# A conformer block on one core: gated unit and conv in 128 + 16 channels, paired scores, and a reordered start

## Chip, cores and metric

One NeuronCore of a Trainium2 chip. The metric is the device time of one execution in microseconds (us), lower is better. "Granted clock" is the share of full speed that TensorE got. The engines are PE (TensorE, matmuls), PEld (its weight loads), ACT (ScalarE), DVE (VectorE), POOL (GpSimd) and SP (SyncE, which issues DMAs here).

## The reference, cut to what matters

```python
B, T, D, K, H = 2, 4000, 144, 5, 4          # bf16 throughout
x = x + 0.5 * silu(ln(x) @ w_ff1a) @ w_ff1b # FF, 576 wide
q, k, v = split(ln(x) @ w_qkv)              # 4 heads of 36
x = x + softmax(q k^T * scale) v @ w_o      # full attention over 4000 tokens
a, b = split(ln(x) @ w_pw1)                 # the gated unit: two halves of 144 channels
h = a * sigmoid(b)
c = sum_i shift(h, i) * dw[i]               # conv over 5 tokens, per channel
x = x + silu(c) @ w_pw2
x = x + 0.5 * silu(ln(x) @ w_ff2a) @ w_ff2b
return ln(x)
```

## The kernel before

Tokens are worked on in 16 chunks of 512 (two of them 416), four blocks of 128 per chunk. The program is written by a small list scheduler in Python: every operation is recorded with an estimated cost, threads of "side work" (FF, projections, gated unit, conv) compete, and the order per engine that comes out is fixed when the kernel is built.

Attention runs as 992 tiles of 128 keys x 512 queries x 2 heads. Most exponentials are on ScalarE; some are computed on VectorE with shifts and a polynomial:

```python
def dve_exp():                              # a VectorE tile
    ...
    for hh in range(2):
        if hh:
            bk = yield need("pe", banks, dur=-0.24)
        s_mm(gi, kt, hh, PSV[:, bk, 0:m], [("ps", bk)], 0.107)   # two 64x64 matmuls of 512 columns
        op("dve", "tensor_scalar", DN[...], PSV[:, bk, 0:m], ...)
        op("dve", "scalar_tensor_tensor", DF[...], ...)
        banks.give(bk)
```

The 144 channels of the gated unit and the conv are worked on as two halves of 72, one channel per row (partition):

```python
def glu(c, s, hf):                          # hf = 0, 1
    ...
    mm2(c, WP1, s, D + hf * HD, D + (hf + 1) * HD, bk, HD, ["WP1"])
    t = yield from tanh(n, bk, HD)          # 72 x 512 on ScalarE
    ...
    mm2(c, WP1, s, hf * HD, (hf + 1) * HD, bk, HD, ["WP1"])
    ...
    op("dve", "scalar_tensor_tensor", out=U[0:HD, c % NU, hf, :, 1:1 + nt], ...)
def conv(c, z, hf, silu):                   # nine matmuls per half, weights are diagonal
    ...
```

The softmax here doesn't subtract the row's maximum and nothing guards it: scores larger than these inputs give would overflow.

Of the kernel before, what the change touches and what calls it, by code (L numbers as in the profile page):

```python
# [6 lines left out]
ALU = mybir.AluOpType  # L7
# [32 lines left out]
class Rec:  # L40
# [7 lines left out]
    def __init__(self, nc):  # L48
        self.nc = nc
        self.ops = []  # L50
        self.n = {}
        self.hist = {}
        self.free = {e: 1.0 for e in self.ENGS}
        self.kind = None
        self.last = 0.0
        self.filler = None

    def op(self, eng, name, *a, r=(), w=(), q=None, cost=0.1, kind=None, **k):
        o = Op()
        o.eng, o.name, o.a, o.k, o.q = eng, name, a, k, q  # L60
        o.deps, o.inc, o.cnt = [], False, 0
        lane = eng if q is None else "q:" + q
        o.idx = self.n.get(lane, 0)
        self.n[lane] = o.idx + 1
        for key in r:
            h = self.hist.setdefault(key, ([], []))
            o.deps += [(d, True) for d in h[0]]
            h[1].append(o)
        for key in w:
            h = self.hist.setdefault(key, ([], []))  # L70
            o.deps += [(d, key[0] in ("DN", "DF", "PD")) for d in h[0] + h[1] if d is not o]
            if h[1] and not (len(h[1]) == 1 and h[1][0] is o):
                self.hist[key] = ([o], [])
            else:
                h[0].append(o)
        start = self.free[eng]
        for d, raw in o.deps:
            if d.eng != eng or d.q is not None or (raw and eng != "pe"):
                start = max(start, d.done)
        if eng == "pe" and kind == "idle":  # L80
            start = self.free["pe"]
        elif eng == "pe":
            gap = start - self.free["pe"]
            if self.filler is not None and gap > 0.3:
                self.fill(int((gap - 0.15) / 0.11), o, lane)
            if kind != self.kind:
                start += 0.13
            self.kind = kind
        self.free[eng] = start + cost
        o.done = start + cost + self.LAT[eng]  # L90
        self.last = o.done
        self.ops.append(o)
        return o
# [186 lines left out]
def bass_standalone__conformer_family_zipformer__speech_kernel(  # L280
# [43 lines left out]
    LEAD = 20  # L324
    NSER = 3
    LATE = 0.8
# [4 lines left out]
    SLACK, MORE, LAG = 0.7, 0.4, 3  # L331
# [24 lines left out]
    U = sb("U", [NU, 2, NB, KTL + 4])  # L356
    SW = sb("SW", [NSW, 2, CH])
# [11 lines left out]
    WP1 = sb("WP1", [2, 2 * D])  # L369
    WP2 = sb("WP2", [2, D])  # L370
    DWR = sb("DWR", [D])
    DWT = sb("DWT", [2, 8], F32)
    DG = sb("DG", [2, KCONV, HD])
# [12 lines left out]
    def load(eng, q, dst, src, w):  # L386
        op(eng, "dma_start", dst, src, q=q, w=w, cost=0.7)
# [19 lines left out]

    load_x("sp", 0)
# [4 lines left out]
    load("sp", "w2", WO[0:HD, :, :], kh(w_o), ["WO"])  # L413
    load("sp", "w2", WP1[0:HD, :, :], kh(w_pw1), ["WP1"])
    load("sp", "w2", WP2[0:HD, :, :], kh(w_pw2), ["WP2"])
    load("sp", "w2", DWR[0:KCONV, :], dw, ["DWR"])
    load_ff("sp", "w2", WA2, WB2, w_ff2a, w_ff2b, "W2")
    for c in range(CPB, NCH):
        load_x("sp", c)

    op("dve", "memset", DUM[:, :], 0.0, w=["DUM"])
    op("pool", "memset", IDENT[:, :], 0.0, w=["ID0"])
# [3 lines left out]
    op("pool", "memset", XN[:, :, :, :, :], 0.0, w=["XN0"], cost=2.0)  # L426
    op("pool", "memset", AN[:, :, :, :, :], 0.0, w=["AN0"], cost=1.0)
    op("dve", "memset", WQ[:, :, :, :], 0.0, w=["WQ0"])
    op("dve", "memset", WK[:, :, :, :], 0.0, w=["WK0"])
    zero_ff(WA1, WB1, "W1")  # L430
    zero_ff(WA2, WB2, "W2")
    op("dve", "tensor_copy", IDF[:, :], IDENT[:, :], r=["ID"], w=["IDF"], cost=0.2)

# [10 lines left out]
    def setup_qk():  # L444
        for Wt, nm, o0 in ((WQ, "WQ", 0), (WK, "WK", D)):
            for k in range(2):
                op("dve", "tensor_copy", Wt[0:HD, k, :, 0:DH],
                   WQKV[0:HD, k, o0:o0 + D].rearrange("p (h d) -> p h d", h=H), r=["WQKV", nm + "0"], w=[nm],
                   cost=0.15)
# [36 lines left out]
    def setup_dw():  # L486
        bk = yield need("pe", banks, dur=0.1)
        for k in range(2):
            op("pe", "transpose", PSH[0:HD, bk, k * 8:k * 8 + KCONV], DWR[0:KCONV, k * HD:(k + 1) * HD],
               IDENT[0:KCONV, 0:KCONV], r=["DWR", "ID"], w=[("ps", bk)], kind="s")  # L490
        yield need("dve")
        op("dve", "tensor_scalar", DWT[0:HD, :, 0:KCONV],
           PSH[0:HD, bk, 0:16].rearrange("p (k n) -> p k n", k=2)[:, :, 0:KCONV], 0.5, None, op0=ALU.mult,
           r=[("ps", bk)], w=["DWT"])
        banks.give(bk)
        for k in range(2):
            yield need("dve")
            for i in range(KCONV):
                op("dve", "tensor_scalar", DG[0:HD, k, i, :], IDENT[0:HD, 0:HD], DWT[0:HD, k, i:i + 1], None,
                   op0=ALU.mult, r=["DWT", "ID"], w=["DG"], cost=0.2)  # L500

# [20 lines left out]
    def transp(c, src, rk, s, g, flat=False):  # L522
# [3 lines left out]
        if not (mode["front"] or mode["tail"] or flat):  # L526
# [3 lines left out]
               src(rows).rearrange("p i k f -> p (i k f)"), q=f"t{s}_{g}", r=rk, w=[("XT", s, g)], cost=0.1)  # L530
# [221 lines left out]
    def glu(c, s, hf):  # L752
        cc = c % CPB
        bk = yield need("pe", banks, dur=0.43)
        n, nt = nc_(c), tb(c)
        mm2(c, WP1, s, D + hf * HD, D + (hf + 1) * HD, bk, HD, ["WP1"])
        t = yield from tanh(n, bk, HD)
        banks.give(bk)
        bk = yield need("pe", banks, dur=0.43)
        mm2(c, WP1, s, hf * HD, (hf + 1) * HD, bk, HD, ["WP1"])  # L760
        yield need("dve")
        op("dve", "scalar_tensor_tensor", out=U[0:HD, c % NU, hf, :, 1:1 + nt],
           in0=TH[0:HD, t, 0:n].rearrange("p (i n) -> p i n", i=NB), scalar=1.0,
           in1=PSV[0:HD, bk, 0:n].rearrange("p (i n) -> p i n", i=NB), op0=ALU.add, op1=ALU.mult,
           r=[("TH", t), ("ps", bk)], w=[("U", c % NU)], cost=0.63)
        banks.give(bk)
        thp.give(t)

    def post1(c, a):
# [20 lines left out]
        if cc == 0:  # L790
            op("pool", "memset", U[0:HD, v, :, 2:4, 0:1], 0.0, w=[("UL", v)], cost=0.1)
        else:
            op("pool", "tensor_copy", U[0:HD, v, :, 2:4, 0:1], U[0:HD, w, :, 2:4, KTL:KTL + 1],
               r=[("U", w)], w=[("UL", v)], cost=0.25)
            op("pool", "tensor_copy", U[0:HD, w, :, 0:2, KTL + 1:KTL + 2], U[0:HD, v, :, 0:2, 1:2],
               r=[("U", v)], w=[("UR", w)], cost=0.25)
        if cc == CPB - 1:
            op("pool", "memset", U[0:HD, v, :, 0:2, n + 1:n + 2], 0.0, w=[("UR", v)], cost=0.1)
        glu_done.add(c)

    def conv(c, z, hf, silu):
        v, n, nt = c % NU, nc_(c), tb(c)
        bk = yield need("pe", banks, dur=1.07)
        o = PSV[0:HD, bk, 0:n].rearrange("p (i n) -> p i n", i=NB)
        u = U[0:HD, c % NU, hf, :, :]
        parts = [(2, 0, 4, 0, 1), (1, 1, 4, 0, 1), (1, 0, 1, 3, 0), (0, 2, 4, 0, 1), (0, 0, 2, 2, 0),
                 (3, 0, 3, 1, 1), (3, 3, 4, 0, 2), (4, 0, 2, 2, 1), (4, 2, 4, 0, 2)]
        for j, (tap, i0, i1, s0, off) in enumerate(parts):
            op("pe", "matmul", o[:, i0:i1, :], lhsT=DG[0:HD, hf, tap, :], rhs=u[:, s0:s0 + i1 - i0, off:off + nt],
               start=j == 0, stop=j == len(parts) - 1, r=[("U", v), ("UL", v), ("UR", v), "DG"], w=[("ps", bk)],  # L810
               cost=0.0525 * (i1 - i0), kind="f", skip_group_check=True)
        if silu:
            yield need("act")
            op("act", "activation", SW[0:HD, z, hf, 0:n], PSV[0:HD, bk, 0:n], ACT.Silu, bias=0.0, scale=1.0,
               r=[("ps", bk)], w=[("SW", z)], cost=0.48)
            banks.give(bk)
            return
        t = yield from tanh(n, bk, HD)
        yield need("dve")
        gate(SW[0:HD, z, hf, 0:n], n, bk, HD, t, [("SW", z)])  # L820
# [3 lines left out]
    def post2(c):  # L824
# [9 lines left out]
        def half(g):  # L834
            yield from residual(
                c, g, lambda i: [(SW[0:HD, z, k, i * n:(i + 1) * n], WP2[0:HD, k, :]) for k in range(2)],
                1.0 if silu else 0.5, [("SW", z), "WP2"])
# [114 lines left out]
    def dve_exp():  # L952
# [4 lines left out]
        while True:  # L957
# [3 lines left out]
            bk = yield need("pe", banks, cond=lambda: stolen() is not None, dur=-0.24)  # L961
# [6 lines left out]
            for hh in range(2):  # L968
                if hh:
                    bk = yield need("pe", banks, dur=-0.24)  # L970
                s_mm(gi, kt, hh, PSV[:, bk, 0:m], [("ps", bk)], 0.107)
# [6 lines left out]
                   cost=0.64)  # L978
# [63 lines left out]
    setup_qk()  # L1042
    for c in range(CPB):
        S.add(ff1(c, True))
# [52 lines left out]
    while n_e < n_s or group() is not None:  # L1097
# [9 lines left out]
        lag = len(att_done) - len(fin)  # L1107
# [4 lines left out]
        if th is not None and (stuck or a is None or t < a or (th.req[0] == "act" and t < a + 0.05)):  # L1112
# [3 lines left out]
            if mode["front"] and len(kv_done) == CPB:  # L1116
                mode["front"] = False
                S.add(setup_dw())
                S.add(series(g for c in range(CPB, NCH) for g in (ff1(c, False), pre2(c))))
# [60 lines left out]
```

## Time and profile before

| what | before |
|---|---|
| runs when first timed | 1069.4, 1081.8, 1082.3 us; profiled run 1072.8 |
| span of the profiled run | 1071.0 us, mean granted clock 0.979 |
| start to first exponential | 55.3 us |
| first to last exponential | 966.4 us |
| last exponential to the end | 49.3 us |

"Middle" below is the second of these stretches, "end" the third; both count from the starts of those exponentials. The view of busy time by stretch gives, for any stretch, its length and each engine's busy us with the instruction count in brackets, in the order PE, PEld, DVE, ACT, POOL, then granted clock, DMA share and GB/s. For the middle of before:

```profile
55.30:1021.70 966.40, 833.11 (x9724) 288.72 (x9724) 674.09 (x1582) 935.08 (x1128) 325.16 (x505) 0.99 0.10 19
```

Subtracting ScalarE's busy time from the length leaves 31.3 us idle: middle = ScalarE's busy time + its idle time.

### The profile page before, as it was taken

The numbers are of one execution on the slowest core, as the hardware profiler recorded it, in microseconds if no ns is written. First come the engines' busy times: TensorE is split into PE (matmuls) and PEld (weight loads), VectorE is DVE, ScalarE is ACT, GpSimd is POOL, SyncE is SP. The second block draws the span as 40 slices with busy tenths as digits, with TensorE's granted clock in tenths as the row PEclk, the third lists the DMA queues.
The fourth block names the chain that finished last, engine by engine and source line by source line (L and its number), as shares of the span: only waits on it lengthen the run. The fifth ranks groups of instructions, "written<-read, shape, count | busy, mean of one in ns | idle before, by whom it ended". The sixth has DMA issues, their size and how long they took to land.

```text
span 1071.0 us, 25080 instructions
## 1 busy us (share of the span) xinstructions
PE 920.2 (86%) x10499; PEld 348.2 (33%) x10499; DVE 745.0 (70%) x1883; ACT 983.2 (92%) x1219; POOL 364.7 (34%) x589
## 2 busy tenths in 40 slices
PE   8998888887989989898888889888888888888886
PEld 4632222222233323233332233322232232333254
DVE  7885378767655675757678886588748877765654
ACT  3698999998999999999999999999999999999952
POOL 5431141404237452653622043520443040515213
PEclk8999999999999999899999999999999999999997
DMA  4000010101012010110100011100101010102000
GB/s 124 2 2 9 13 31 11 26 6 26 16 26 41 19 39 11 26 34 13 31 7 19 1 26 21 27 14 7 25 17 27 1 31 1 27 11 32 12 2 16
DMA packets 76089, 22.29 MB, mean 21 GB/s; under 512 B 73400, under 2 KB 75976, under 8 KB 75976
## 3 DMA queue, kind: packets, MB, share of 16 engines
q1 hardware_dynamic: 74820, 20.22, 9.4%
q8 instruction: 82, 1.34, 0.5%
q10 hardware_dynamic: 1156, 0.47, 0.2%
q14 instruction: 31, 0.25, 0.1%
HBM read 3.30 MB, written 2.30 MB: 5 GB/s over the span
## 4 chain that ended last, share of the span: by engine, by line
ACT 62%; PE 24%; DVE 5%; DMA 3%; POOL 2%; issue 2%; SPq 1%; ACTq 0%; POOLq 0%; DVEq 0%
ACT PT L161 55%; PE PS L161 24%; ACT TH L161 5%; DMA XT<-AN 2%; POOL RS L161 1%; DVE PD L161 1%; ACT HT L161 1%; POOL XN L161 1%; DMA XT<-XN 1%; DVE XN L161 1%; SPq L161 1%; DVE ST L161 1%; DMA WQKV<-in_w_qkv_dram 0%; ACT PR L161 0%; DVE DF L161 0%
## 5 line engine op out<-in xcount | busy, mean ns | idle before, releaser
L161 ACT ACTIVATE PT<-PS 128x1024 bf16<-128x1024 f32 (+1 forms) x932 | 870.0, 1050 | 18.5 <-PE PS L161 16.2
L161 PE MATMUL PS<-QT,KT 64*64 64x512 bf16 (+1 forms) x3968 | 416.7, 396 | 100.7 <-ACT PT L161 90.5
L161 PE MATMUL PS<-PT,VA 64*64 64x512 bf16 (+1 forms) x3728 | 362.3, 377 | 0.6 <-ACT PT L161 0.6
L161 PEld LDWEIGHTS PS<-QT,KT 64*64 64x64 bf16 x3968 | 118.7, 104 | 430.4 <-ACT PT L161 358.9
L161 POOL TENSOR_SCALAR RS<-MV 128x2 f32<-128x2 f32 (+1 forms) x160 | 37.2, 232 | 622.4 <-DVE MV L161 622.3
L161 POOL TENSOR_SCALAR XN<-X,MV,RS 128x144 bf16<-128x144 bf16 (+1 forms) x228 | 203.2, 904 | 5.7
L161 POOL TENSOR_TENSOR RS<-RS,NHALF 128x2 f32<-128x2 f32 (+1 forms) x160 | 115.3, 721 | 13.3
L161 PEld LDWEIGHTS PS<-PT,VA 64*64 64x64 bf16 x3728 | 111.1, 107 | 21.2 <-issue 11.2
L161 DVE SCALAR_TENSOR_TENSOR HT<-TH,PS 128x512 bf16<-128x512 bf16 (+2 forms) x105 | 64.5, 622 | 66.6 <-ACT TH L161 66.4
L161 ACT ACTIVATE TH<-PS 128x512 bf16<-128x512 f32 (+4 forms) x165 | 99.6, 604 | 10.1 <-PE PS L161 9.3
L161 PE MATMUL PS<-XT,WA 72*128 72x512 bf16 (+3 forms) x384 | 91.5, 356 | 13.5 <-issue 6.2
L161 DVE TENSOR_SCALAR DN<-PS 128x512 bf16<-128x512 f32 (+1 forms) x120 | 80.7, 679 | 29.0 <-PE PS L161 27.4
L161 DVE SCALAR_TENSOR_TENSOR X<-PS,X 128x288 bf16<-128x288 f32 (+1 forms) x128 | 57.1, 447 | 41.2 <-PE PS L161 40.8
L161 DVE TENSOR_TENSOR PD<-PD,DF 128x1024 f16<-128x1024 f16 (+1 forms) x120 | 83.2, 694 | 3.6
L161 DVE SCALAR_TENSOR_TENSOR DF<-PS,DN 128x512 f16<-128x512 f32 (+1 forms) x120 | 81.6, 683 | 3.6
L161 DVE BATCH_NORM_STATS2 ST<-X 128x6 f32<-128x144 bf16 (+1 forms) x320 | 81.3, 296 | 3.0
L161 PE MATMUL PS<-WB,HT 128*128 128x144 bf16 (+1 forms) x640 | 51.3, 233 | 2.1 <-ACT HT L161 1.2
L161 PEld LDWEIGHTS PS<-XT,WA 72*128 72x128 bf16 x384 | 29.9, 100 | 70.9 <-issue 33.9
L161 DVE COPY OTA<-PS 128x512 f32<-128x512 f32 (+1 forms) x32 | 21.7, 679 | 40.4 <-PE PS L161 40.4
L161 PEld LDWEIGHTS PS<-WB,HT 128*128 128x128 bf16 (+1 forms) x640 | 42.5, 105 | 19.5 <-issue 5.7
L161 DVE BATCH_NORM_AGGREGATE MV<-ST 128x2 f32<-128x6 f32 (+1 forms) x320 | 44.5, 169 | 0.0
L161 DVE TENSOR_TENSOR PD<-PD,DN 128x1024 uint16<-128x1024 f16 (+1 forms) x60 | 42.8, 719 | 1.7
(76 smaller groups left out, 685.9 us busy)
## 6 DMA issues: line engine op xcount, KB each, us to landing
X<-in_x_dram SPq DMA_DIRECT2D x14, 144.0 KB, 3.3
out_dram<-XN SPq DMA_DIRECT2D x28, 72.0 KB, 1.7
XT<-XN SPq DMA_TRANSPOSE x86, 2.4
XT<-AN SPq DMA_TRANSPOSE x30, 2.5
X<-in_x_dram SPq DMA_DIRECT2D x2, 117.0 KB
out_dram<-XN SPq DMA_DIRECT2D x4, 58.5 KB
WA<-in_w_ff1a_dram ACTq DMA_DIRECT2D x1, 144.0 KB
WB<-in_w_ff1b_dram ACTq DMA_DIRECT2D x1, 144.0 KB
```

The lines of the kernel that those rows point to most:

```text
L161: ins = getattr(eng, o.name)(*o.a, **o.k)
```

## The change

Its intent: columns are what costs and rows next to nothing, so 144 channels go as one pass of 128 rows and one pass in which the last 16 channels of four token blocks are stacked at rows 0, 32, 64 and 96, 128 columns long. The scores of a VectorE tile are issued together, so that all four 64x64 tiles of the array work at once. The first norms no longer stand behind the copies of the QKV weights. With them came new scheduler constants: LEAD (the fewest tiles left in a group that VectorE may take one from), LATE (the lateness that this needs), MORE (slack per lag), NPRE (series in which the second batch is prepared) and AHEAD (how far that runs ahead). The core of the diff:

```diff
-    def glu(c, s, hf):
+    def glu(c, s, rem):
+        if rem:                                   # 16 channels x 4 blocks
+            for k in range(2):
+                for j, w0 in enumerate((2 * D - 16, 128)):
+                    for i in range(NB):
+                        op("pe", "matmul", PSV[32 * i:32 * i + 32, bk, 256 * j:256 * j + nt], ...)
+        else:
+            mm2(c, WP1, s, D, D + 128, bk, 128, ["WP1"])
...
+        if rem:                                   # the conv of the stacked 16 channels
+            n = nt
+            for sh in range(3):
+                op("pe", "matmul", PSV[:, bk, 0:n], lhsT=DR[:, sh, :], rhs=U[:, v, NB, sh:sh + nt], ...)
+        else:                                     # nine matmuls with diagonals of 128 x 128
...
-            bk = yield need("pe", banks, cond=lambda: stolen() is not None, dur=-0.24)
+            bk = yield need("pe", banks, cond=lambda: len(banks.free) > 1 and stolen() is not None, dur=-0.24)
+            bks = (bk, banks.take())
...
-        if not (mode["front"] or mode["tail"] or flat):
+        dma = not (mode["front"] or mode["tail"] or flat)
+        if mode["front"] and not flat and c:
+            yield need("sp")
+            dma = R.free["sp"] < max(R.ready(k) for k in rk) + 0.3
...
-               src(rows)..., q=f"t{s}_{g}", r=rk, w=[("XT", s, g)], cost=0.1)
+               src(rows)..., q=f"t{s}_{g}", r=rk, w=[("XT", s, g)], cost=1.2)
...
-    LEAD = 20                  LATE = 0.8              MORE = 0.4
+    LEAD = 18    NPRE = 2      LATE = 0.2  AHEAD = 0.6 MORE = 0.2
...
-    setup_qk()
     for c in range(CPB):
-        S.add(ff1(c, True))
+        S.add(ff1(c, True), ready=R.ready(("X", c, 0)))
+    S.add(setup_qk(), ready=R.ready("WQKV"))
```

Cut: the buffers, the padded weights, smaller fills, the silu table loaded early, the float32 identity copied later, the weights and second half of x loaded after the start.

## The prediction

> **What bounds the kernel now.** I first read the page's busy shares, then cut the span into three stages with the view of busy time by stretch. The columns there are stretch, length, then busy us and (count) of each engine, the granted clock, the DMA share and GB/s.
>
> ```profile
> PE 920.2 (86%) x10499; PEld 348.2 (33%) x10499; DVE 745.0 (70%) x1883; ACT 983.2 (92%) x1219; POOL 364.7 (34%) x589
> ...
> 0.00:100.00 100.00, 90.69 (x824) 46.97 (x824) 76.12 (x321) 69.02 (x110) 35.64 (x74) 0.97 0.13 34
> 100.00:1010.00 910.00, 784.42 (x9188) 271.88 (x9188) 640.46 (x1453) 884.23 (x1061) 315.69 (x484) 0.99 0.10 20
> 1010.00:1071.00 61.00, 45.05 (x495) 29.37 (x494) 28.37 (x110) 29.99 (x50) 13.37 (x31) 0.88 0.03 8
> ```
>
> The overall 92% of ScalarE hides three regimes. From 100 to 1010 us ScalarE is busy 884.2 of 910 us, 97.2%: it is the bound, and only 25.8 us of idle time are left there. In the first 100 us it is busy 69.0 us, and at the end about half. The waits of ScalarE inside the middle stage (us in total, times, longest) say who is to blame for the rest:
>
> ```profile
> ACT PT L161 <- PE PS L161: 16.2, 32, 2.4
> ACT TH L161 <- PE PS L161: 6.5, 15, 0.8
> ```
>
> 22.7 of the 25.8 us are waits for TensorE. The groups by form say what ScalarE does, and what VectorE pays for the gates:
>
> ```profile
> L161 ACT ACTIVATE PT<-PS 128x1024 bf16<-128x1024 f32 x812 | 776.4, 1070 | 17.2 <-PE PS L161 15.5
> L161 ACT ACTIVATE PT<-PS 128x832 bf16<-128x832 f32 x120 | 94.0, 919 | 1.3 <-PE PS L161 0.8
> L161 ACT ACTIVATE TH<-PS 72x512 bf16<-72x512 f32 x54 | 33.4, 618 | 4.8 <-PE PS L161 4.1
> L161 DVE SCALAR_TENSOR_TENSOR U<-TH,PS 72x512 bf16<-72x512 bf16 x28 | 19.1, 684 | 28.5 <-PE PS L161 25.3 <-ACT PT L161 3.1
> L161 DVE TENSOR_SCALAR PD<-DF 128x1024 f16<-128x1024 f16 x56 | 24.5, 440 | 1.6
> ```
>
> There are 992 exponential tiles (32 groups of 31); ScalarE does 812 + 120 = 932, VectorE the other 60. A full ScalarE tile occupies 776.4/812 = 0.96 us of its time, 0.92 in an unbroken run. So three things shorten the middle: less other ScalarE work, more tiles on VectorE, fewer waits for TensorE. VectorE is idle there for 910 - 640 = 270 us, so it is not the bound.
>
> The start is bound otherwise. From the timeline of the first 15 us (start, duration, engine, instruction, what ended the idle time before it):
>
> ```profile
> 1.44 3.51 POOL L161 MEMSET XN<- 128x4096 bf16 x1
> 2.56 4.21 DVE L161 CAST IDF<-IDENT 128x128 f32<-128x128 bf16 x1
> 4.89 1.81 POOL L161 MEMSET AN<- 128x2048 bf16 x1
> 8.73 0.30 DVE L161 COPY WQ<-WQKV 72x144 bf16<-72x144 bf16 x2 [1.29 <-DMA WQKV<-in_w_qkv_dram]
> 9.17 0.51 DVE L161 BATCH_NORM_STATS2 ST<-X 128x6 f32<-128x144 bf16 x2
> 11.64 0.41 PE L161 MATMUL PS<-IDENT,XN 128*72 128x128 bf16 x4 [0.68 <-DVE XN L161]
> 14.54 3.83 PE L161 MATMUL PS<-XT,WA 72*128 72x512 bf16 x12 [0.29 <-issue]
> ```
>
> The first norm (9.17) stands in VectorE's program behind a cast that takes 4.21 us and a copy that waits for the QKV weights. The data were there before: loads of x take 3.3 us in the median and the first is issued at 0.72, so it landed near 4. After that the first blocks repeat every 4.29 us (first silu of a block at 22.40, 26.69, 30.98, 35.27), and between 20 and 40 us TensorE is busy 19.4 of 20 us: there it is the bound.
>
> **What the Trainium skill says.** "ScalarE: Activation LUTs", section What ACT_TABLE_LOAD costs, gives 186 ns + 0.833 ns per column for an ACTIVATE with immediates, 93 ns of which overlap back to back: 0.95 us for 1024 columns and 0.52 for 512. The chain shows 0.92 and 0.49, so I take its slope with the trace's slots. "SBUF — State Buffer", section Who interferes with whom: the port pair that VectorE's 2-port copies and GpSimd share is an exclusive lock, and the loser waits. The trace fits: the cast of 128 columns ends at 6.77, GpSimd's second fill at 6.70. "TensorE: Matmul & The Clock Gate", section Wait — 56ns, not 53.3ns?: start to start is columns/2.4 GHz + 2.5 ns, 0.216 us for 512 columns, 0.056 for 128. A conv half (9 matmuls, 2560 columns, so 1.09 us) shows 1.06 us of weight loads in the last stage. "TensorEngine Tiling (Array Packing)", section Key Properties: tiles of one array run in parallel, a change of tiling drains. The trace shows four 64x64 score matmuls of 512 columns in 0.41 us from first start to last end, so they do overlap.
>
> **The change part by part.**
>
> *Channels 128 + 16 on ScalarE.* Each of 16 chunks has a gated unit and a conv, each with two activations of 72 rows x 512 columns. They become one of 128 x 512 and one of 128 x 128. Rows are free, columns cost: a slot of 0.49 us for 512 columns shrinks to 0.49 - 384 x 0.000833 = 0.17. A pair goes from 0.98 to 0.66, 0.32 saved, x32 pairs = 10 us, some 28 pairs (9 us) in the middle stage, where ScalarE is the bound and all of it counts.
>
> *The same on VectorE.* A gate of 512 columns is 0.684 us. The rows of HT give 0.683 for 512 and 0.420 for 256, so about 0.29 for 128; a pair saves 0.395, x about 30 = 12 us. VectorE isn't the bound, so this only buys tiles: a tile costs VectorE 2 x 0.686 + 2 x 0.689 + 0.440 + 0.446 + 2 x 0.702 + 0.723 = 5.8 us, so two tiles.
>
> *The same on TensorE.* Conv: 18 matmuls (2.13 us of weight loads in the trace) become 9 and 3 of 128 columns: 1.06 + 0.17, saving 0.9 us x 16 = 14 us. Gated unit: 8 x 0.216 become 4 x 0.216 and 16 narrow ones of 128 columns, 0.22 us if four run side by side, 0.9 if none do: between 0 and 0.65 us x 16, say 5 us. The output product keeps its two terms.
>
> *Paired scores.* A VectorE tile's scores were two pairs of matmuls at different times, two tiles of the array idle each time; now all four go together, 0.43 to 0.22 us, x60 = 13 us of TensorE, and one change of tiling less. The price is that both banks left for side work must be free at once, and the second is held while VectorE works on the first (1.4 us more).
>
> TensorE thus loses some 32 us. None is on ScalarE's clock directly; it reaches the end through the 22.7 us of waits and by letting side work and VectorE tiles in earlier. I take 6 us of the waits.
>
> *More VectorE tiles.* The bar for starting one falls (lateness 0.8 to 0.2, least remaining 20 to 18), TensorE has room, VectorE has 270 idle us. The pairing speaks against it. I choose 60 to about 68: 8 x 0.93 = 7 us, from VectorE's share of the middle rising from 70% to about 74%.
>
> *The start.* The norm goes from 9.17 to about 4.5: fills of 1.65 and 0.9 us of VectorE remain before it and x lands near 4. TensorE can't use all of it: its 36 warm-up matmuls run to 10.96. Transposes go from 11.64 to about 10.9, but then all are ready instead of arriving over 2 us, so the first FF matmul goes from 14.54 to about 12: 2.5 us. The silu table (1.28 us at 14.68) is loaded earlier, perhaps 0.5 us more. Some transposes of later blocks go to DMA: eight on TensorE cost 0.61 us per block in the trace, 14 such sets in the front; if half move, 4 us where TensorE is the bound. The start is worth 7 us.
>
> *The end.* From the last exponential at 1022.8 to 1071 is a chain of single blocks. It holds 2.1 us of conv matmuls in front of the last transposes and two more conv pairs: 3 us.
>
> *Moved loads and two series.* Late weights and the second half of x are issued after the front instead of at 5 to 13 us. They fill the SP queue by some 25 issues x 0.43 us, 10 us around 90 us, when the first transposes of the next stage want it. I charge 1 us.
>
> Sum: 9 + 6 + 7 + 7 + 3 - 1 = 31 us off the profiled span of 1071, so 1040. The runs of before, 1069.4 to 1082.3 with 1072.8 for the profiled one, lie some 6 us over the span on average; 1046 it is, 3% under their mean of 1076.7.
>
> **Rivals.** *The pairing starves side work.* Only two banks serve side work, and a paired tile holds both for its first 1.5 us. Then the tile count stays at 60 or falls, and TensorE's gain becomes waits for banks. For it: those waits already exist (27 us of VectorE waiting before DN). Against: the scheduler asks for both banks free before it starts. Outcome: 1058 to 1064. *TensorE's gain goes straight to the end.* The chain that ended last is PE for 24%, so one might take 24% of 1071 as TensorE-bound and expect 50 us. Against: the same stretches have ScalarE at 96 to 98% busy, so the chain there merely passes through TensorE. Outcome if true: 1025. *VectorE takes many tiles.* At 80% busy, 18 more: 10 us better, 1036. *The start is hidden by the warm-up and weights.* Then its gain is 1 or 2 us: 1051.
>
> **Range and chances.** The firm parts are 9 us of activations, about 3 of the start and 3 of the end: 15 us, 1.4%. Passing 2% (1055) needs some 7 more from tiles, waits and transposes, which I put at 16. I give that 0.74, 0.25 to within 2%, 0.01 to slower. The range is 1028 to 1064.
>
> **What would show it.** In the profile after: 128x128 activations and gates in place of the 72-row ones, ScalarE's time for TH down by some 9 us; PT count down from 932 to about 924; first norm near 4.5 and first FF matmul near 12 us; block period in the front under 4.29 us; conv matmuls 12 per chunk; ScalarE still at 97% or more in the middle. I am wrong if PT goes up, if ScalarE's waits for TensorE grow over 25 us, or if the first exponential comes no earlier than 55.3 us.

## More of the kernel before

Normed blocks are transposed by a DMA issued from SP; the scheduler's estimate of its queue time stands at the end of the line:

```python
op("sp", "dma_start_transpose", XT[:, s, ...], src(rows)..., q=f"t{s}_{g}", r=rk, w=[("XT", s, g)], cost=0.1)
```

## The result, and the profile after

The changed kernel ran at 1030.8, 1034.2 and 1037.1 us in its fast runs (1054.6 in one slow run, at granted clock 0.959, left out); before had a median of 1082.0 over four runs. The ratio is 0.9594 (95% interval 0.948 to 0.971). Every ratio here is the mean of one kernel's fast runs over the mean of before's fast runs of the same rounds, so it is not quite the ratio of quoted medians. The result is correct. The forecast was 1046 us with a range of 1028 to 1064.

The profiled span fell from 1071.0 to 1029.0 us, by 42 us against 31 forecast. The middle of the changed kernel, busy time by stretch as above:

```profile
48.10:988.50 940.40, 797.90 (x9807) 272.30 (x9807) 686.22 (x1645) 922.52 (x1122) 333.17 (x510) 0.99 0.11 23
```

ScalarE is busy 922.5 us (12.6 less than before) and idle 17.9 (13.4 less). The waits of ScalarE for TensorE in this stretch, to be set against the 16.2 and 6.5 us of before (the same in before's whole middle as in the prediction's window):

```profile
ACT PT L165 <- PE PS L165: 8.4, 25, 1.4
ACT TH L165 <- PE PS L165: 3.0, 10, 0.7
```

The account by stretch of the profiled runs:

| stretch | before | after | difference | forecast |
|---|---|---|---|---|
| start to first exponential | 55.3 | 48.1 | -7.2 | -7 |
| middle, ScalarE busy | 935.1 | 922.5 | -12.6 | -16 |
| middle, ScalarE idle | 31.3 | 17.9 | -13.4 | -6 |
| end | 49.3 | 40.5 | -8.8 | -3 |
| moved loads | | in the rows above | | +1 |

The start, from the timeline of the changed kernel (start, duration, engine, instruction, idle time before it and what ended it):

```profile
1.17 9.67 PE L165 MATMUL PS<-DUM 128*128 128x512 bf16 x36 [1.17 <-DVE DUM L165]
...
3.97 0.52 DVE L165 BATCH_NORM_STATS2 ST<-X 128x6 f32<-128x144 bf16 x2
...
10.68 0.61 PE L165 MATMUL PS<-IDENT,XN 128*72 128x128 bf16 x8
...
12.24 2.34 PE L165 MATMUL PS<-XT,WA 72*128 72x512 bf16 x12 [0.50 <-ACT XT L165]
```

The first norm stands at 3.97 us instead of 9.17, the first FF product at 12.24 instead of 14.54. As foreseen, it is the 36 warm-up matmuls that hold it there.

What the split into 128 + 16 channels saves can be read without any contention in the gated unit of the very last chunk (416 tokens). The timeline of before:

```profile
1035.29 0.92 ACT L161 ACTIVATE TH<-PS 72x416 bf16<-72x416 f32 x2 [0.63 <-PE PS L161]
...
1036.45 1.08 DVE L161 SCALAR_TENSOR_TENSOR U<-TH,PS 72x416 bf16<-72x416 bf16 x2
...
1037.88 2.01 PE L161 MATMUL PS<-U,DG 72*72 72x416 bf16 x18
```

and of the changed kernel:

```profile
1001.13 0.67 ACT L165 ACTIVATE TH<-PS 128x416 bf16<-128x416 f32 x2 [0.62 <-PE PS L165]
...
1002.31 0.76 DVE L165 SCALAR_TENSOR_TENSOR U<-TH,PS 128x416 bf16<-128x416 bf16 x2
...
1003.43 1.08 PE L165 MATMUL PS<-U,DG 128*128 128x416 bf16 x9 [0.91 <-POOL U L165]
...
1004.35 0.30 PE L165 MATMUL PS<-U,DR 128*128 128x104 bf16 x3
```

Two activations of 416 columns became one of 416 and one of 104 (the line names only the first shape): 0.92 to 0.67 us, and by the slope of the prediction 312 columns x 0.000833 = 0.26 was due. The gate fell by 0.32 us, the conv matmuls from 2.01 to 1.22 us (first start to last end).

VectorE tiles went from 60 to 65 (exponentials on ScalarE from 932 to 927), where 68 were expected.

The same can be read for the whole middle, by the groups of ScalarE's activations by form, before and then after:

```profile
L161 ACT ACTIVATE TH<-PS 128x512 bf16<-128x512 f32 x76 | 49.1, 646 | 4.0 <-PE PS L161 3.9
L161 ACT ACTIVATE TH<-PS 72x512 bf16<-72x512 f32 x52 | 32.2, 619 | 2.6 <-PE PS L161 1.9
...
L165 ACT ACTIVATE TH<-PS 128x512 bf16<-128x512 f32 x105 | 68.9, 656 | 3.2 <-PE PS L165 2.7
L165 ACT ACTIVATE TH<-PS 128x128 bf16<-128x128 f32 x27 | 9.5, 350 | 0.0
```

Neighbours overlap, so I counted each activation in the traces from the end of the one before it. The gated unit and the conv then cost 27.4 us for 28 pairs before and some 19.5 for 29 pairs after: 0.98 and 0.67 us a pair, where the prediction has 0.98 and 0.66. The exponentials fell from 842.5 to 839.4 us, ScalarE's copies (QT, KT, VA, XT) from 9.8 to 6.9, and the FF's tanh, two more of them, rose by 1.4. These four, -7.9, -3.1, -2.9 and +1.4, make up the 12.6 us to 0.1.

### The profile page after: what moved, and what is told of

It reads as the page before. It is cut to its first block, busy times and chain, and to the rows that moved or that the text cites. A ratio compares the mean times of both kernels' runs of the same rounds, so it can differ in the third digit from the quotient of the medians.

```text
span 1029.0 us, 25199 instructions
## 1 busy us (share of the span) xinstructions
PE 871.0 (85%) x10488; PEld 321.4 (31%) x10488; DVE 749.9 (73%) x1938; ACT 963.6 (94%) x1202; POOL 369.7 (36%) x594
## 4 chain that ended last, share of the span: by engine, by line
ACT 67%; PE 25%; DVE 5%; issue 1%; POOL 1%; DMA 1%; POOLq 0%; DVEq 0%; ACTq 0%; SPq 0%
ACT PT L165 60%; PE PS L165 25%; ACT TH L165 6%; POOL RS L165 1%; ACT HT L165 1%; DVE HT L165 1%; DVE DF L165 1%; DVE PD L165 0%; DVE ST L165 0%; DVE DN L165 0%; DMA XT<-AN 0%; ACT KT L165 0%; DVE X L165 0%; DVE XN L165 0%; DVE DR L165 0%
## 5 line engine op out<-in xcount | busy, mean ns | idle before, releaser
L165 PE MATMUL PS<-QT,KT 64*64 64x512 bf16 (+1 forms) x3968 | 403.4, 393 | 118.5 <-ACT PT L165 104.8
L165 PEld LDWEIGHTS PS<-QT,KT 64*64 64x64 bf16 x3968 | 115.5, 103 | 441.8 <-ACT PT L165 371.0
L165 POOL TENSOR_SCALAR XN<-X,MV,RS 128x144 bf16<-128x144 bf16 (+1 forms) x232 | 206.2, 901 | 6.8
L165 DVE SCALAR_TENSOR_TENSOR HT<-TH,PS 128x512 bf16<-128x512 bf16 (+3 forms) x110 | 67.7, 623 | 84.0 <-ACT TH L165 83.9
L165 PEld LDWEIGHTS PS<-PT,VA 64*64 64x64 bf16 x3708 | 111.4, 106 | 20.5 <-issue 8.7
L165 ACT ACTIVATE TH<-PS 128x512 bf16<-128x512 f32 (+4 forms) x170 | 97.3, 573 | 6.0 <-PE PS L165 5.4
L165 PE MATMUL PS<-XT,WA 72*128 72x512 bf16 (+3 forms) x384 | 89.3, 348 | 13.1 <-DVE HT L165 9.6
L165 DVE TENSOR_SCALAR DN<-PS 128x512 bf16<-128x512 f32 (+1 forms) x130 | 87.3, 672 | 16.8 <-PE PS L165 10.3
L165 DVE TENSOR_TENSOR PD<-PD,DF 128x1024 f16<-128x1024 f16 (+1 forms) x130 | 88.5, 680 | 3.7
L165 DVE SCALAR_TENSOR_TENSOR DF<-PS,DN 128x512 f16<-128x512 f32 (+1 forms) x130 | 87.6, 674 | 4.1
L165 DVE COPY OTA<-PS 128x512 f32<-128x512 f32 (+1 forms) x32 | 21.7, 679 | 32.9 <-PE PS L165 32.9
```

The source lines that it names most:

```text
L165: ins = getattr(eng, o.name)(*o.a, **o.k)
```

## The experiments

The forecast of the sum was low, in two terms: ScalarE's idle time and the end. **Theory W** says ScalarE's work and a few waits set the time; **theory P** (called L later) that TensorE's saved time is what counts; **theory O** that the new constants brought the surplus. A fourth, **theory Q**, came from looking where before had lost its 31 us, and the prediction had passed over it: one number in the diff, `cost=0.1` to `cost=1.2`.

Before, at 263 us, TensorE did nothing for 2.31 us. The timeline there (SPq is SP's queue of DMA issues):

```profile
258.94 6.05 SPq L161 DMA_TRANSPOSE XT<-XN  x3
...
263.48 0.59 PE L161 MATMUL PS<-XT,WK 72*128 72x512 bf16 x2 [2.31 <-issue]
...
264.46 1.94 ACT L161 ACTIVATE PT<-PS 128x1024 bf16<-128x1024 f32 x2 [2.43 <-PE PS L161]
```

A projection (XT,WK) had been put into TensorE's program ahead of the next scores, as if its transposes were done. The views by tile give the transposes of XN 1.19 us of queue each in the median, over 86 of them, and 2.4 us to landing. The scheduler believed 0.1 us. The next scores stand behind the projection in TensorE's program (they start at 264.00 us), so they waited too, and ScalarE for them. The profile names "issue" as the cause of the 2.31 us; the view of tile XN for this stretch lists the same 2.3 us under those who waited for its transposes. The next lines (busy time by stretch) show what follows:

```profile
262.00:263.40 1.40, 0.00 (x0) 0.00 (x0) 1.33 (x3) 0.03 (x1) 1.40 (x2) 1.00 0.13 28
263.40:266.80 3.40, 3.33 (x24) 0.90 (x28) 1.40 (x3) 1.94 (x2) 3.17 (x6) 0.64 0.49 43
```

After the stop the granted clock drops to half for a few us, TensorE is full, and ScalarE waits again: 1.94 of 3.40 us busy.

The table is needed by all that follows. Columns 2 to 5 are us of the profiled run; "stops" are gaps of TensorE over 0.95 us between 100 and 1000 us (the fifth of after, at 997.7 us, is already in its end). "Half clock" is for the stretches of 3.41 us that lie wholly between 110 and 985 us: twice the sum of (1 - granted clock) x 3.41. It leaves out the first 50 us or so of the middle, where some runs lost more: over the whole middle it is 23.9 us for before, 10.2 for after, 81.9 for e4, 51.2 for e9, 27.3 for e1, 23.9 for e10 and e11, 20.5 for e7.

| run | first exp. at | middle busy | middle idle | end | VectorE tiles | stops | half clock | ratio (95%) |
|---|---|---|---|---|---|---|---|---|
| before | 55.3 | 935.1 | 31.3 | 49.3 | 60 | 7 | 23.9 | 1 |
| after | 48.1 | 922.5 | 17.9 | 40.5 | 65 | 5 | 3.4 | 0.959 (0.948-0.971) |
| e1_old_consts | 49.2 | 926.3 | 25.9 | 44.5 | 59 | 6 | 3.4 | 0.964 (0.958-0.970) |
| e2_before_new_consts | 51.9 | 925.5 | 47.6 | 59.4 | 72 | 8 | 56.7 | 0.999 (0.993-1.004) |
| e3_old_gate | 48.9 | 923.0 | 20.1 | 49.5 | 68 | 2 | 0.0 | 0.965 (0.960-0.970) |
| e4_no_pair | 47.7 | 921.9 | 41.4 | 46.6 | 66 | 4 | 20.5 | 0.971 (0.965-0.977) |
| e5_before_pair | 55.7 | 935.4 | 30.6 | 49.3 | 62 | 7 | 13.6 | 0.998 (0.993-1.002) |
| e6_before_tr_cost | 55.4 | 927.7 | 17.6 | 51.1 | 63 | 3 | 0.0 | 0.986 (0.980-0.992) |
| e7_pad | 48.9 | 921.9 | 26.2 | 44.3 | 67 | 3 | 6.3 | 0.974 (0.967-0.980) |
| e8_old_front | 54.6 | 926.3 | 25.0 | 38.3 | 65 | 5 | 20.5 | 0.969 (0.964-0.975) |
| e9_tr01 | 44.0 | 924.5 | 41.6 | 46.9 | 66 | 9 | 31.6 | 0.992 (0.986-0.997) |
| e10_late025 | 47.9 | 922.7 | 22.1 | 44.5 | 64 | 2 | 11.3 | 0.962 (0.957-0.968) |
| e11_before_pair_tr | 52.9 | 934.1 | 26.3 | 46.6 | 61 | 1 | 6.8 | 0.988 (0.983-0.992) |
| e12_warm20_one_series | 46.4 | 920.9 | 29.8 | 38.2 | 68 | 4 | 17.1 | 0.971 (0.964-0.977) |

All outputs are right. The 12 runs came in three batches of four, each on another chip; before's medians there were 1081.9, 1076.0 and 1073.7 us, so I compare ratios and not microseconds across batches. All columns but tiles and ratio come from one execution each.

Two counts from these traces sort the runs by `cost`. Stops in front of a product that reads a transposed block (XT), ending 0.04 to 0.14 us after a transpose landed: 6 to 8 in each of the four runs with 0.1 (before, e2, e5, e9), 0 to 2 in each of the ten with 1.2. ScalarE's idle time from 110 to 985 us: 24.8, 35.5, 23.9 and 30.0 us in the four, 11.5 (after) to 19.1 in nine of the ten; e12 is the exception with 26.1.

### e1_old_consts: the structure with the old constants

```diff
-LEAD = 18; NPRE = 2; AHEAD = 0.6; LATE = 0.2; MORE = 0.2
+LEAD = 20; NPRE = 1; AHEAD = -100.0; LATE = 0.8; MORE = 0.4
```

> The changed kernel with the scheduling constants of before (lateness 0.8, least remaining 20, slack per lag 0.4, no running ahead, one series for the second batch). The program then holds 59 VectorE tiles instead of 65 and ends with 19 silu activations after the last exponential instead of 14. Theory W (ScalarE's work in the middle sets the time): 6 tiles x 0.93 us + some 4 us at the end, so 1042 to 1048 us against 1034 for the fast runs of after. Theory O (the order, retuned, brought most of what exceeded the forecast): 1055 or more. Theory P (TensorE's saved work itself brought it): 1038 or less, since TensorE's work is the same.

Measured: 1043.8 us median, ratio 0.964, against 0.959 of after with overlapping intervals. The first of the three expectations holds: the constants are worth about half a per cent here (six tiles and one FF at the end), though not clear of noise. Theory O falls for the bulk.

### e2_before_new_consts: the constants alone

```diff
-LEAD = 20; LATE = 0.8; MORE = 0.4         # one series
+LEAD = 18; NPRE = 2; AHEAD = 0.6; LATE = 0.2; MORE = 0.2
```

> The kernel of before with only the new scheduling constants and the two series. It holds 72 VectorE tiles instead of 60, but 24 silu activations are left after the last exponential instead of 19. Theory W: 12 tiles x 0.93 = 11 us less in the middle, up to 5 us more at the end: 1068 to 1074 against some 1077 of before. Theory O: 1060 or less. Theory P: no better than 1075.

Measured: 1080.8 us, ratio 0.999. Missed by theories W and O, on the slow side; only theory P's "no better than 1075" is met. ScalarE's busy time fell by 9.6 us as expected from 12 tiles, but idle time rose by 16 and the end by 10. More VectorE tiles alone buy nothing.

### e3_old_gate: gated unit and conv as before

```diff
-    def glu(c, s, rem): ... U[:, c % NU, 0:NB, ...], SW[:, z, CH:CH + n], WP2[:, i, :]
+    def glu(c, s, hf): ...  U[0:HD, c % NU, hf, ...], SW[0:HD, z, hf, ...], WP2[0:HD, k, :]
```

> The changed kernel with gated unit, conv and output product of before (two halves of 72 channels); all else as after. Theory W: 28 pairs of activations x 0.32 = 9 us of ScalarE in the middle come back, minus 3 tiles more on VectorE (68), plus 2 to 5 us at the end: 1041 to 1048. Theory P: about 19 us of TensorE come back and show nearly whole: 1052 or more.

Measured: 1043.9 us, ratio 0.965. In the expected range of theory W, and below theory P's 1052: TensorE's busy time in the middle rose by 12 us and ScalarE's idle time by only 2. But the 9 us did not come back where I expected: the middle's busy time is the same, since three more tiles are on VectorE and nine tanh activations fewer are in it (156 instead of 165). That work sits in the end instead, 49.5 us against 40.5. The gated unit's and the conv's own activations in the middle do take 27.1 us here against some 19.5 (counted as above): the term itself is there, and other work made room for it.

### e4_no_pair: the scores of a VectorE tile one bank at a time

```diff
-            bks = (bk, banks.take())
-                s_mm(gi, kt, hh, PSV[:, bks[hh], 0:m], [("ps", bks[hh])], 0.0535)
-            for hh, bk in enumerate(bks):
+                if hh:
+                    bk = yield need("pe", banks, dur=-0.24)
+                s_mm(gi, kt, hh, PSV[:, bk, 0:m], [("ps", bk)], 0.107)
```

> The changed kernel with the scores of a VectorE tile in two separate pairs of matmuls, one bank at a time, as before; 66 tiles. Theory W: 1 to 4 us slower than after through waits (1035 to 1039). Theory P: 66 x 0.21 = 14 us slower (1046 or more). The rival that pairing starves side work of banks: faster than after, 1031 or less, with waits of VectorE before DN down.

Measured: 1049.6 us, ratio 0.971. Theory P's number, and not what I expected. ScalarE's work is the same as after's (921.9 and 922.5 us), all of the loss is idle time. That pairing starves side work of banks is refuted: the unpaired kernel is the slower one, and VectorE waited longer in front of its steps that read scores (DN), 21.7 us against 10.3. Part of this profile's idle time is not pairing, though. From about 49 to 109 us this execution ran at half clock; busy time by stretch, the unpaired kernel:

```profile
60.00:80.00 20.00, 20.00 (x108) 5.06 (x106) 10.25 (x44) 13.09 (x16) 4.65 (x10) 0.50 0.22 42
```

the changed kernel:

```profile
60.00:80.00 20.00, 18.61 (x185) 6.50 (x184) 14.30 (x52) 17.64 (x23) 4.65 (x10) 1.00 0.41 96
```

The first step of a VectorE tile in this run starts at 161.0 us, later than this, so the form of their scores can't be the cause. Of the 23.5 us more idle time than after's, 16.9 lie before 110 us; from 110 to 985 us it is 18.0 us against 11.5 (and 14.2 in e10). The three timed runs beside it were faster (1048.4 to 1050.6 us at granted clock 0.974; the profiled one 1059.4 at 0.957), and still slower than after. Whether they too lost the clock early isn't on record.

### e5_before_pair: pairing alone

```diff
+            bks = (bk, banks.take())          # in the kernel of before, as in the change
```

> The kernel of before with only the paired scores (62 VectorE tiles, two more than before). The run without pairing was 12 us slower than the changed kernel, with the same ScalarE work in the middle (921.9 against 922.5 us) but 41 instead of 18 us of ScalarE idle, and a lower granted clock. Theory L (less TensorE time, hence fewer and shorter waits of ScalarE): 1067 to 1073 against some 1081 of before, ScalarE's idle time between first and last exponential down from 31 to 20 us, fewer stretches at half clock. Theory N (that run's loss came from its own order and from a stretch at half clock after the start, not from pairing): 1077 or more. Starved banks: 1082 or more.

Measured: 1072.9 us, ratio 0.998 with 1 inside the interval. Theory N's side. TensorE's busy time in the middle fell by 11 us (833.1 to 822.4), ScalarE's idle time by 0.7. TensorE's saved time was worth nothing here, next to seven stops that remained.

### e6_before_tr_cost: one number of the scheduler

```diff
-  q=f"t{s}_{g}", r=rk, w=[("XT", s, g)], cost=0.1)
+  q=f"t{s}_{g}", r=rk, w=[("XT", s, g)], cost=1.2)
```

> The kernel of before with one number of its scheduler changed as in the change: the queue time of a DMA transpose 1.2 us instead of 0.1. In before, TensorE stood up to 2.31 us at 263 us in front of a product whose transpose was the third in a row on the queue. Theory Q (part of the unforeseen gain is side work no longer placed ahead of its transposes): 1070 to 1075, stops of TensorE over 0.95 us fewer than 7. Theory L: 1078 to 1084, no change.

Measured: 1061.8 us (1053.7 to 1065.5), ratio 0.986: 1.4% from a number that changes no instruction's form, more than expected. The middle in busy time by stretch:

```profile
55.40:1000.70 945.30, 818.99 (x9676) 281.57 (x9675) 675.73 (x1583) 927.73 (x1118) 314.36 (x489) 1.00 0.10 19
```

Idle time of ScalarE 17.6 us, as in the changed kernel, stops 7 to 3, half clock 23.9 to 0 us. Busy time fell by 7.4 as well: three tiles more on VectorE and one FF pushed into the end, which is 1.8 us longer.

### e7_pad: pairing kept, its TensorE time given back

```diff
+            op("pe", "matmul", PSV[:, bks[0], :], lhsT=DUM[:, 0:128], rhs=DUM[:, :], start=True, stop=True,
+               r=["DUM"], w=[("ps", bks[0])], cost=0.215, kind="f")    # overwritten by the scores
```

> The changed kernel with one useless matmul of 512 columns per VectorE tile, 67 in all, ahead of the paired scores: TensorE's time of the unpaired form comes back (67 x 0.216 = 14.5 us), banks and pairing stay. The program also ends with 19 silu activations instead of 14, worth up to 4 us. Theory L: 1043 to 1052, the same as without pairing (1049.6), with the clock lower than after's. Rival T (it is the form, two tiles of the array instead of four, that costs): 1034 to 1040.

Measured: 1047.0 us, ratio 0.974 (one slow run at 1068.8 left out). Theory L's range: a kernel with a useless matmul per tile ran as slowly as the unpaired one, 0.974 and 0.971. That speaks for TensorE's time and against the form, but not clear of noise: against e10 (0.962), with the same end, it is 1.1% with intervals that just overlap, and in the profiled runs 4.1 us of idle time.

### e8_old_front: the start as before

```diff
-    S.add(setup_qk(), ready=R.ready("WQKV"))   # and: partial fills, late IDF, late loads, silu preload, DMA transposes
+    setup_qk()                                 # ahead of the norms, whole fills, IDF early, all loads first
```

> The changed kernel with the start of before: whole fills, the early cast, norms behind the QKV weights, all loads first, no silu preload, transposes of the start on TensorE; the same 65 VectorE tiles and the same end. Forecast of the start: 7 us, so 1040 to 1044 against some 1036; the first exponential near 55 us instead of 48.1. Rival (hidden by warm-up and weights): 1 or 2 us.

Measured: 1044.1 us, ratio 0.969 against 0.959. The first exponential is at 54.6 instead of 48.1 us: 6.5 us, the forecast's 7. Some of the 6.5 us is the clock and not the path: this execution, like those of before, e5 and e6, spent 6.8 us at half clock from about 15 us on, that of after none. What that is worth can be seen in before, e2 and e11, which run the same instructions on TensorE and ScalarE up to the first exponential: it comes at 55.3 us in before, and at 51.9 and 52.9 in e2 and e11, where the clock stayed up. Busy time by stretch, before and e11:

```profile
12.00:32.00 20.00, 18.17 (x144) 12.54 (x144) 14.88 (x69) 12.24 (x24) 8.50 (x19) 0.83 0.12 37
12.00:32.00 20.00, 17.21 (x173) 12.29 (x174) 16.84 (x78) 13.47 (x27) 9.92 (x21) 1.00 0.12 35
```

The rest of this profile's loss is in the middle, where ScalarE was idle 25.0 us with 20.5 us at half clock.

### e9_tr01: the number undone in the changed kernel

```diff
-  q=f"t{s}_{g}", r=rk, w=[("XT", s, g)], cost=1.2)
+  q=f"t{s}_{g}", r=rk, w=[("XT", s, g)], cost=0.1)
```

> The changed kernel with the scheduler's queue time of a DMA transpose set back from 1.2 to 0.1 us; 66 VectorE tiles, 19 silu activations after the last exponential. In the kernel of before the same number alone brought 1.4% and took ScalarE's idle time in the middle from 25 to 12 us. Theory Q (that number is the unforeseen gain): 1046 to 1054, ratio to before 0.972 to 0.98, ScalarE's idle time between 110 and 985 us at 20 us or more. If the other parts make it needless: 1036 to 1042, of which 4 from the end.

Measured: 1066.7 us (1058.9 to 1070.5), ratio 0.992. Four fifths of the whole gain are gone, more than theory Q expected. The middle in busy time by stretch:

```profile
44.00:1010.10 966.10, 817.33 (x9800) 277.48 (x9800) 691.71 (x1654) 924.48 (x1118) 326.19 (x506) 0.97 0.11 22
```

ScalarE's work is 2.0 us above the changed kernel's, and 41.6 us are idle. TensorE stops nine times for over 0.95 us, and seven of the nine stand in front of a product that reads a transposed block and end when one lands (XT,WP five times, XT,WA and WO,XT once each). Two of them, from the timeline:

```profile
265.83 0.42 PE L165 MATMUL PS<-WO,XT 72*128 72x144 bf16 x4 [1.19 <-DMA XT<-AN]
...
277.61 1.01 PE L165 MATMUL PS<-XT,WP 72*128 72x512 bf16 x2 [1.93 <-issue]
```

The start is the best of all, 44.0 us, where the scheduler then sends more transposes to DMA (19 against 16 in the first 50 us); the middle, 25.7 us longer, eats those 4.1 us six times over.

### e10_late025: a control of the order

```diff
-LATE = 0.2
+LATE = 0.25
```

> Control of the order: the changed kernel with one constant off by little (lateness 0.25 instead of 0.2), 64 VectorE tiles, 19 silu activations after the last exponential as in the runs without pairing and with the useless matmul. If chance in the order is small: 1038 to 1042 (4 from the end, 1 from a tile), and pairing is worth the distance to the unpaired run, 8 to 11 us. If chance in the order is as large as these effects: anywhere up to 1050, and the pairing's worth can't be told.

Measured: 1035.9 us, ratio 0.962 (one slow run at 1048.2 left out), after's within the intervals. A small push to the order moves the time by 0.3% and brings one FF back into the end, so a difference of 0.9% (e4 against this run, with the same activations at the end) is more than order alone in this one trial. One control is a thin base; I call pairing's worth in the changed kernel likely, at 0.9 to 1.2% and not more, and not shown, since e4 also lost the clock early.

### e11_before_pair_tr: pairing on the sound order

```diff
+            bks = (bk, banks.take())
-  cost=0.1)
+  cost=1.2)
```

> The kernel of before with paired scores and the queue time 1.2 us, 61 VectorE tiles, 19 silu activations after the last exponential. The queue time alone gave a ratio of 0.986, with 63 tiles and 24 silu activations. Theory L (pairing takes waits away once the order is sound): 0.976 to 0.981. If pairing brings nothing: 0.984 to 0.988.

Measured: 1062.2 us, ratio 0.988, beside 0.986 of the number alone. "Brings nothing": this order has two tiles fewer and one FF more in the middle (busy 934.1 against 927.7 us). So pairing seemed worth something only in the changed kernel. Why there and not here is open; that the new constants, which ask more of TensorE through VectorE tiles, are the condition was not tested. Of this profile's 26.3 us of idle time, 11.8 come before 110 us (5.6 of e6's 17.6), where this execution ran 17 us at half clock.

Beside e5 this run is a second trial of the number alone, on the paired kernel: 0.988 against 0.998, seven stops became one, and ScalarE's idle time from 110 to 985 us went from 23.9 to 14.2 us. Busy time by stretch, e5 and then this run:

```profile
110.00:985.00 875.00, 745.35 (x8803) 257.77 (x8800) 626.45 (x1412) 851.12 (x1016) 297.23 (x459) 0.99 0.11 20
110.00:985.00 875.00, 750.05 (x8950) 258.84 (x8946) 631.22 (x1426) 860.84 (x1030) 304.93 (x465) 1.00 0.11 20
```

### e12_warm20_one_series: a try to beat the change

```diff
-NWARM = 36; NPRE = 2
+NWARM = 20; NPRE = 1
```

> A try to beat the changed kernel: 20 warm-up matmuls instead of 36, since the chain that ended last runs through them until 10.9 us while the first normed block is ready at 6.4; and one series for the second batch, which gives 68 VectorE tiles and the same end. First transposes near 7 us, first exponential at 44 to 45 us instead of 48.1 if the weights have landed and the clock stays up, 48 if not; middle 2 to 3 us less by three tiles. In all 1029 to 1034, ratio 0.953 to 0.957.

Measured: 1043.1 us, ratio 0.971. It doesn't beat the changed kernel. Sixteen warm-ups fewer brought the first exponential only from 48.1 to 46.4 us: in this execution the matmuls ran at the slow pace of 0.43 us until 7.1 us, and the 20 were done at 8.6. The middle had 68 tiles and the least ScalarE work of all, 920.9 us, and lost it to 29.8 us of idle time. I found no version that beats the changed kernel.

## Why the prediction was right or wrong, point by point

- **The total.** 1034.2 us (median of the fast runs; 1035.7 with the slow one) lies in the range of 1028 to 1064, and "faster by over 2%" was given 0.74. The gain was under-forecast: 31 us of span against 42. (Two of the prediction's readings are off by 0.1 us, to no effect: the mean of the four runs of before is 1076.6, and the last exponential ends at 1022.7.)
- **The bound.** Right. ScalarE is busy 98.1% of the middle after (922.5 of 940.4 us), and in every run of the table its busy time is at least 95% of the middle.
- **128 + 16 channels.** Right: 9 us taken for the middle, 7.9 measured with one pair more in it (0.31 us a pair of 0.32), and 0.25 us of 0.26 for the last gated unit. What the total gains by it is less plain: undoing it (e3) lengthened the end by 9 us and the middle by 3, because the order lets side work slip.
- **More VectorE tiles.** Direction right, size off: 5 instead of 8, and 3.1 us instead of 7, since those that left ScalarE were on balance short ones (the exponentials of 832 columns went from 120 to 114, those of 1024 from 812 to 813). e1 with 59 tiles shows that they come from the constants and not from VectorE's freed time: the new structure with old constants has one tile fewer than before.
- **The start.** The path is right, warm-ups included; that the size came out, 7.2 us against 7, is in part luck. The prediction's own line shows the first 12 FF products of before taking 3.83 us, against 2.34 after: that execution ran at half clock for 6.8 us from 15.2 us on, which the prediction overlooked. Against the same start at full clock (e2 and e11, first exponential at 51.9 and 52.9 us, shown under e8) the new start is worth 3.8 to 4.8 us. The eighth block's first silu comes at 39.6 us after and 44.7 in e11, against 12.9 and 15.7 for the first block: 3.8 us per block instead of 4.1.
- **Waits of ScalarE for TensorE.** This is the term that was most mis-sized: 6 us taken, 13.4 measured as idle time (11.3 of them in the two waits shown). Its reasoning was wrong too. I let the waits shrink with TensorE's load. They shrink when side work stops standing in front of transposes that have not landed: e6, with TensorE's work unchanged in form, takes 13.7 us of idle time away; e5, with 11 us less TensorE time, takes 0.7. The prediction did not mention the changed `cost`. e9 confirms it from the other side: without it the other parts together give 0.8%. e11 beside e5 repeats it on the paired kernel, and the stops that end with a transpose's landing sort all 14 kernels by it.
- **The rival "the pairing starves side work".** Refuted by e4. **"TensorE's gain goes straight to the end"** was set aside for good reason in before (e5: 11 us less of TensorE, nothing gained). In the changed kernel some 14 us of TensorE time were likely worth about 1% (e7, e4). That it counts once the stops are gone is not shown: in e11 they are gone too, and it brought nothing.
- **The end.** 3 us taken, 8.8 measured; the part foreseen came out, and the rest is luck of the order. The ends vary with the gate, with the silu activations left after the last exponential, and with the clock granted there. With 19 left and the old gate it takes 49.3 us at a clock of 0.85 (before, e5) and 46.6 at 0.97 (e11, with as many instructions as the other two on every engine); with the new gate 46.6 to 46.9 at 0.87 to 0.90 (e4, e9) and 44.3 to 44.5 at 0.95 to 0.98 (e1, e7, e10). At like clock the new gate is thus worth 2 to 3 us. With 14 left it is 40.5 at 0.87 (after) and 38.2 at 0.95 to 0.97 (e8, e12): the other 6 us are one FF that was begun before the last exponential, with tanh on ScalarE in place of silu. No part of the prediction looked for it, and it isn't sure to come: the new constants are in e4, e7 and e9 too, and e10 differs by 0.05 in one of them, and these four leave 19. The count alone doesn't set the end either: with 24 left it took 49.5 (e3), 51.1 (e6) and 59.4 us (e2).
- **Moved loads.** One us was charged; nothing of it could be seen. In after the loads hold SP's queue from 68.7 to 79.8 us, and the next transpose is issued at 91.2 us, when the norm that it reads is ready.

How a stop costs more than its own length is, in part, argued. "TensorE: Matmul & The Clock Gate", section What's actually happening, says that the clock falls to half after an idle window of about 3.4 us. The trace of before fits that in timing, though not as an idle window: ahead of each loss of clock in its middle stands a stretch of 3.41 us in which TensorE was busy only 1.1 to 2.2 us. That e6 has no stretch at half clock and e9 31.6 us is measured; how much of the idle time is the stop and how much the slow clock after it was not separated.

## What to carry to other kernels

When a program's order is made from estimated costs, an estimate is part of the kernel: compare each with the duration in the trace, the queue time of DMAs first, for one number that was 1.19 us in the trace and 0.1 in the source was worth 1.4% alone, 1.0% beside the pairing and 3% inside the change. When an engine is 97% busy, split its stretch into busy and idle before counting saved work, since here the variants differed by 15 us in work and by 30 in idle time. Parts of a change don't add up: pairing was worth nothing in the kernel of before, with the stops or without them, and likely about 1% in the changed one. Compare one-execution profiles at like clock: the same instructions reached the first exponential at 51.9 us in one run and 55.3 in another.

## What the Trainium skill lacked or had wrong

- "DMA: Bandwidth & Descriptors", section DMA Transpose (X-bar): lists constraints but no issue time; the page's only such figures are cycle counts for other shapes, in its part on a later chip. The runs show 1.19 us on SP's queue for each transpose of a normed half chunk (86 in before, 110 in after) and 2.4 us from issue to landing.
- "TensorE: Matmul & The Clock Gate", section What's actually happening: gives half clock after an idle window. In before the window was not idle: TensorE was busy 1.1 to 2.2 of 3.41 us ahead of a loss of clock. A later section of the page does tell of short idle times that make the clock swing, without saying how busy TensorE was.
- The same section: says that a busy window of about 3.4 us brings the full clock. In e4_no_pair the clock stayed at half from about 49 to 109 us with TensorE busy 20.00 of 20.00 us (60 to 80 us). The page's caveats know of a clock stuck that long, but at a lower rate.
- The same section: its warm-up of about 3.4 us was about that in the profile of after (full pace from 4.6 us, first matmul at 1.2), but in e12_warm20_one_series the slow pace lasted until 7.1 us, 5.9 us after the first matmul.
- No page that I read has how far the mean granted clock of one kernel moves from run to run: the unpaired kernel took 1048.4 us at 0.974 and 1059.4 at 0.957.
